# Joined score stacks, other store and load routes, and rings by lifetime in a gated attention and channel-mixing kernel

## The chip, the cores and the metric

The kernel runs on one core of a Trainium2 chip. The core has a matrix engine (PE, with its weight loads shown as PEld), three engines for elementwise work (DVE, ACT, POOL), a queue engine (SP) that here only issues transfers, and 16 DMA engines between the chip's memory and the core's buffer. Each engine works through its own instructions in order and waits on semaphores for the others.

The metric is the device time of one execution in microseconds (us), from the runs listed below; lower is better.

## The reference, cut to what matters

One sequence of 2048 rows of 512 goes through two branches, and a gate from the row itself mixes them:

```python
g = sigmoid((x * gate_w).sum(-1, keepdims=True))
# a: attention, 32 heads of 16, each row sees itself and the 255 rows before it
qkv = x @ wqkv                     # 512 -> 3 * 512
scores = q @ k.T * 16 ** -0.5      # masked to 0 <= i - j < 256
a = softmax(scores) @ v @ wo
# b: layernorm, 512 -> 1792, gelu, 1792 -> 512
b = gelu(layernorm(x) @ w1 + b1) @ w2 + b2
out = g * a + (1 - g) * b
```

All inputs are float32. The kernel multiplies in a reduced float32 form and makes up for it by splitting each operand into a high and a low part: a product is high x high + high x low + low x high, three matmuls instead of one.

## The kernel before

The kernel has three stages, and the order of every engine's instructions is the order in which the Python text emits them. A step counter drives it: `after(k, fn)` puts `fn` off by k steps, `tick()` advances by one and runs what is due. Every transfer but a few goes through SP's queue, in the order of emission.

**First stage (to about 146 us).** q, k and v are computed from x. q and k go to memory as *stacks* (`qk_out`): per head 50 rows of 2048 columns, 16 rows each of high, high and low parts for q and of high, low and high parts for k, so that one matmul over 48 rows gives the three-part product; two more rows (`gaps`) hold ones for k and later the negative row maximum, in two parts, for q. For three of the four head groups one of the two high copies is made later by a transfer from memory to memory (`double`, line 318). Row statistics, the gate and the normalized input of the second branch (`load_y`) are made here too.

**Second stage (to about 488 us).** The string `ORDER` fixes how four kinds of work alternate on PE: `S` (`s_pair`, line 353: scores, whose maximum DVE takes on line 367), `T` (`st_pair`, line 393: scores again, transposed, with the maximum subtracted inside the matmul; ACT takes exp on line 408, POOL masks on line 410), `P` (`pv`, line 417: the product with v, stored to `osc`), and `f` (`fill`: one pair of matmuls of `mlp1_unit`, line 611, the second branch's first product, stored to `hp`). Eight passes p take four heads each, as two couples `pr` of two heads. A pass has 16 blocks of 128 columns; `block(p, kb)` starts each with a tick. The stacks of a pass lie in four tiles, `qs[0]`, `qs[1]`, `ks[0]`, `ks[1]`, and are overwritten in place: every second block `load_stacks` (line 342) loads 256 columns for the next pass, one transfer for each of the four. `put_max` (line 372) sends four blocks' maxima through memory into the q tiles, in four transfers. The weights of `mlp1_unit` come with `load_w1`; `turn_w1` (line 542) makes a copy with the halves of the partitions exchanged. When no `T` is left, the late stores of `pv` and `mlp1_unit` (lines 440 and 641) go through ACT's queue instead of SP's.

Near the end of this stage `early_w2` loads the first four of 14 tiles of w2 and splits them, and two tiles of `hp` are loaded.

**Output stage (from about 488 us).** 56 items, four chunks of 512 rows by 14 tiles of the hidden layer: `mlp2` (line 840) does 12 matmuls for each (line 847). Ahead of them `load_h`, gelu on ACT and the split on DVE (line 686), and in the first chunk `load_w2`. Once in a chunk `attn_out` (line 797) loads the attention rows and the broadcast reciprocal sums (`rd`) for each of four groups (line 803), scales on POOL (line 806), splits, and multiplies with wo in four groups of 12 matmuls (line 824); ACT and DVE add the gate and the bias (826, 827). `mlp2` adds the second branch and stores (854, 856). Buffers come from two rings of tiles of 2 KB a partition: `e` (6) for the first loads, then one ring `t` (37) for everything, in order of request. The buffers of this stage lie over those of the second: a new tile waits for the last user of what lay there.

Of the kernel before, what the change touches and what calls it, by code (L numbers as in the profile page):

```python
# [49 lines left out]
LAG = 6  # L50
WARM = 10
# [13 lines left out]
def gated_mix_kernel(ctx, tc: tile.TileContext, xt, x2, wqk, wv, wo, xa, gw, w1, w2, b1, b2, out):  # L65
# [25 lines left out]
    def t2(dt=F32, shape=(128, 512)):  # L91
        return get("work", "t" if nt[0] > 0 else "e", abs(nt[0]), shape, dt)
# [59 lines left out]
    qkd = {(g, t): dram.tile([HG, 50, S], F32R, name=f"qk{g}_{t}") for g in range(NG) for t in range(2)}  # L152
# [4 lines left out]
    qs = [get("ring", f"q{j}", 1, (128, S), F32R) for j in range(2)]  # L157
    ks = [get("ring", f"k{j}", 1, (128, S), F32R) for j in range(2)]
# [42 lines left out]
    def gaps(g):  # L201
        for t in range(2):
            sp.dma_start(f32(view(qkd[g, t], [50 * S, HG], [S, 2], [1, S], off=48 * S)), f32(ks[0][112:128]))
# [100 lines left out]
    def qk_out(g, t, c, o):  # L304
        d = qkd[g, t]
# [4 lines left out]
        def send():  # L310
            for k, src in ((0, h), (1 + t, h), (2 - t, l)):
                if src is l or k == 0 or g == 0:
                    sp.dma_start(f32(view(d, [S, DH], [50 * S, HG], [1, C], off=k * DH * S + c * C)), f32(src))
            done.add(("qk", g, t, c))
# [3 lines left out]
    def double(g, c):  # L318
        for t in range(2):
            fr, to = (f32(view(qkd[g, t], [S, DH], [50 * S, HG], [1, C], off=k * DH * S + c * C)) for k in (0, 1 + t))  # L320
            sp.dma_start(to, fr)
# [20 lines left out]
    def load_stacks(p, a, n):  # L342
# [3 lines left out]
        for pr in range(2):  # L346
            for t, dst in ((1, ks[pr]), (0, qs[pr])):
                src = view(qkd[g, t], [S, 98], [1, n], off=(4 * j + 2 * pr) * 50 * S + a)
                sp.dma_start(f32(dst[14:112, a:a + n]), f32(src))
# [22 lines left out]
    def put_max(p, a):  # L372
# [8 lines left out]
        def rest():  # L381
            done.add(("m", p, a // 4))
            for pr in range(2):
                for e in range(2):
                    src = view(md, [2048, 2], [1, 512], off=(2 * pr + e) * 512)
                    sp.dma_start(f32(qs[pr][62 + 50 * e:64 + 50 * e, a * 128:a * 128 + 512]), f32(src))
# [30 lines left out]
    def pv(p, j, last):  # L417
# [17 lines left out]
        if j % 2:  # L435
# [3 lines left out]
            else:  # L439
                act.dma_start(to, s)  # L440
# [101 lines left out]
    def turn_w1(i):  # L542
        w1t[i, 1] = [wt(), wt()]
        for k in range(2):
            for e in range(2):
                sp.dma_start(f32(w1t[i, 1][k][64 * e:64 * e + 64]), f32(w1t[i, 0][k][64 - 64 * e:128 - 64 * e]))
        after(2, lambda: done.add(("w", i, 1)))
# [382 lines left out]
```

## Time and profile before

| what | value |
|---|---|
| median of 3 runs | 699.79 us (696.93 to 700.55) |
| the profiled execution | 699.06 us, span 697.3 us |
| granted PE clock, mean | 0.994 |
| PE busy | 682.1 us, 98% of the span |
| DVE, ACT, POOL busy | 466.0, 367.0, 273.6 us |
| moved by DMA | 137.95 MB, 198 GB/s |

Below, PE is the matmuls and PEld the weight loads; `out<-in` names the tiles; `[0.46 <-ACT t L131]` at a row's end is the idle time before it and what ended it; SPq and ACTq are issues of transfers by those queues. In the list of waits the three numbers are the total, how many, and the longest. In the chain of waits a row is a start, a duration and what ran or was in flight. The profile draws a matmul until its last result is out, so consecutive ones overlap; their pace is seen in their starts.

### The profile page before, as it was taken

How to read it: one execution, taken by the hardware profiler on the slowest of the kernel's cores; microseconds unless marked ns; L12 is line 12 of the kernel's file. 1: busy time of each engine (PE TensorE's matmuls, PEld its weight loads, DVE VectorE, ACT ScalarE, POOL GpSimd, SP SyncE). 2: the span in 40 equal slices, each digit the busy share in tenths (PEclk: the TensorE clock that was granted, in tenths of full speed). 3: DMA queues.
4: the chain of work that ended last, by engine and by line, in shares of the span. 5: the costliest groups of instructions: out<-in, count | busy, mean ns of one | idle time of the engine just before them, and what ended most of it. 6: DMA issues, size and time to landing. Idle time of an engine off the chain costs nothing.

```text
span 697.3 us, 16311 instructions
## 1 busy us (share of the span) xinstructions
PE 682.1 (98%) x5738; PEld 544.2 (78%) x5738; DVE 466.0 (67%) x1489; ACT 367.0 (53%) x586; POOL 273.6 (39%) x549
## 2 busy tenths in 40 slices
PE   9999999999999999999999999999988999999997
PEld 7877777877787778787887777787766888888885
DVE  5378865897887767767878778774574742824632
ACT  6332223367677576677767678778543322323221
POOL 7210029736465545566546457567020020020110
PEclk9999999999999999999999999999999999999999
DMA  8899876975776775568764655716883561641711
GB/s 271 265 310 303 287 247 227 302 219 169 246 220 199 239 218 163 171 216 265 197 197 148 207 171 162 216 64 220 295 246 102 161 190 50 210 141 50 244 45 60
DMA packets 91446, 137.95 MB, mean 198 GB/s; under 512 B 14852, under 2 KB 38596, under 8 KB 91236
## 3 DMA queue, kind: packets, MB, share of 16 engines
q1 hardware_dynamic: 90068, 135.20, 61.4%
q10 hardware_dynamic: 1296, 1.70, 0.7%
q8 instruction: 45, 0.74, 0.4%
q14 instruction: 37, 0.30, 0.1%
HBM read 81.53 MB, written 54.28 MB: 195 GB/s over the span
## 4 chain that ended last, share of the span: by engine, by line
PE 84%; DMA 9%; DVE 3%; ACT 2%; issue 1%; SPq 0%; POOL 0%; ACTq 0%; DVEq 0%; POOLq 0%
PE ps_b L623 21%; PE ps_a L847 17%; PE ps_b L425 12%; PE ps_d L300 9%; PE ps_b L406 7%; PE ps_o L824 6%; PE ps_b L362 6%; PE ps_d L336 4%; DMA t<-rd 3%; DMA t<-in_wo 2%; DMA t<-in_xa 1%; DMA q<-qk 1%; DMA t<-in_wqk 1%; PE ps_d L285 1%; DMA qk<-t 1%
## 5 line engine op out<-in xcount | busy, mean ns | idle before, releaser
L367 DVE CUSTOM_DVE_ANT_0 scr<-ps_b,wide 128x384 bf16<-128x384 f32 (+1 forms) x472 | 227.7, 530 | 67.8 <-PE ps_b L362 65.5
L623 PE MATMUL ps_b<-x,w 64*128 64x512 f32 x1344 | 209.8, 394 | 0.7 <-DVE t L128 0.7
L410 POOL TENSOR_SCALAR_AFFINE_SELECT p<-p 128x256 f32<-128x256 f32 x368 | 139.9, 411 | 130.1 <-ACT p L408 128.3
L408 ACT ACTIVATE p<-ps_b 128x768 f32<-128x768 f32 x192 | 146.6, 795 | 32.3 <-PE ps_b L406 25.3
L847 PE MATMUL ps_a<-x,t 128*128 128x512 f32 x648 | 150.0, 390 | 0.7 <-DVE t L686 0.5
L847 PEld LDWEIGHTS ps_a<-x,t 128*128 128x128 f32 x648 | 121.4, 188 | 27.4 <-ACT t L682 0.9
L623 PEld LDWEIGHTS ps_b<-x,w 64*128 64x128 f32 x1344 | 129.1, 187 | 10.2 <-DVE t L128 1.1
L406 PE MATMUL ps_b<-q,k 64*128 64x384 f32 (+5 forms) x512 | 90.1, 345 | 0.2 <-DVE mx L367 0.2
L806 POOL TENSOR_TENSOR t<-t,t 128x512 f32<-128x512 f32 x16 | 22.4, 1402 | 159.2 <-DMA t<-rd 121.7
L362 PE MATMUL ps_b<-k,q 62*128 62x384 f32 (+3 forms) x472 | 82.5, 338 | 2.3 <-DMA q<-qk 2.3
L131 ACT ACTIVATE t<-ps_b 128x256 f32<-128x256 f32 (+1 forms) x116 | 53.1, 487 | 46.6 <-PE ps_b L425 35.0
L425 PE MATMUL ps_b<-p,v 128*32 128x256 f32 (+1 forms) x1472 | 71.8, 330 | 0.0
L128 DVE TENSOR_TENSOR t<-t,t 128x512 fp32r<-128x512 f32 x66 | 49.6, 757 | 27.3 <-ACT t L131 24.1
L406 PEld LDWEIGHTS ps_b<-q,k 50*128 50x128 f32 (+1 forms) x512 | 49.4, 184 | 16.7 <-DVE mx L367 3.8
L425 PEld LDWEIGHTS ps_b<-p,v 128*32 128x32 f32 x1472 | 42.4, 110 | 23.3 <-issue 3.3
L362 PEld LDWEIGHTS ps_b<-k,q 62*128 62x128 f32 (+1 forms) x472 | 47.0, 186 | 13.3 <-issue 2.9
L410 POOL TENSOR_SCALAR_AFFINE_SELECT xq<-xq 128x256 f32<-128x256 f32 x112 | 43.2, 410 | 23.2 <-ACT xq L408 22.3
L408 ACT ACTIVATE xq<-ps_b 128x768 f32<-128x768 f32 (+1 forms) x64 | 44.3, 706 | 14.9 <-PE ps_b L406 13.0
L824 PE MATMUL ps_o<-wo,t 128*128 128x512 f32 x192 | 47.3, 399 | 4.1 <-ACT t L131 4.1
L827 DVE SCALAR_TENSOR_TENSOR us<-b2s,g,us 128x512 f32<-128x512 f32 x16 | 12.0, 752 | 58.5 <-ACT us L826 58.5
L682 ACT ACTIVATE t<-t,b1s 128x512 f32<-128x512 f32 x52 | 35.7, 714 | 22.4 <-DMA t<-hp 22.4
L131 ACT ACTIVATE t<-ps_d 128x512 fp32r<-128x512 f32 x32 | 18.9, 595 | 53.4 <-PE ps_d L300 44.5
(91 smaller groups left out, 734.0 us busy)
## 6 DMA issues: line engine op xcount, KB each, us to landing
qk<-t SPq DMA_DIRECT2D x72, 256.0 KB
hp<-t SPq DMA_DIRECT2D x54, 256.0 KB
t<-hp SPq DMA_DIRECT2D x52, 256.0 KB
k<-qk SPq DMA_DIRECT2D x112, 98.0 KB
q<-qk SPq DMA_DIRECT2D x112, 98.0 KB
osc<-t SPq DMA_DIRECT2D x30, 256.0 KB
w<-w SPq DMA_DIRECT2D x28, 256.0 KB
t<-in_w SPq DMA_DIRECT2D x26, 256.0 KB
```

Of the source, the lines that this page charges most:

```text
L128: eng.tensor_tensor(out=lo, in0=src, in1=f32(hi), op=ALU.subtract)
L131: act.activation(dst, src, AF.Copy)
L300: pe.matmul(o, a[:, dt * 128:(dt + 1) * 128], b[:, dt * C:(dt + 1) * C], start=n == 0, stop=n == 11)
L362: pe.matmul(o[:, e, :n], qs[pr][r:k, qb * 128:qb * 128 + 128], ks[pr][r:k, t0:t0 + n], start=True, stop=True)
L367: dve.tensor_tensor_reduce(out=sc[:, :n], in0=o[:, e, :n], in1=wide[:, 384 - n:], scale=1.0, scalar=NEG, op0=ALU.add, op1=ALU.max, accum_o ...
L406: pe.matmul(o[:, e, :w], ks[pr][r:k, kb * 128:kb * 128 + 128], qs[pr][r:k, kb * 128:kb * 128 + w], start=True, stop=True)
L408: act.activation(pt[:, :, :w], o[:, :, :w], AF.Exp, scale=0.25)
L410: pool.affine_select(out=pt[:, :, a:a + 128], in_=pt[:, :, a:a + 128], pattern=[[0, 2], [sgn, 128]], base=b, channel_multiplier=-sgn, comp ...
L425: pe.matmul(a[32 * h:32 * h + 32, at:at + w], vs[:, kb, v:v + 32], pts[p, kb][:, h, fr:fr + w], start=n == 0, stop=n == len(parts) - 1, sk ...
L623: pe.matmul(o[:, e], w[kt // 4][r:r + 64, k, m:m + 128], y[r:r + 64, a:a + C], start=n == 0, stop=n == 23)
L824: pe.matmul(a, hl[g][x][:, b * 128:b * 128 + 128], wos[g][:, k], start=n == 0, stop=n == 11)
L847: pe.matmul(accs[c][b], x[:, b * 128:(b + 1) * 128], w, start=f == 0 and n == 0, stop=f == FT - 1 and n == 2)
```

## The change

- q and k of both couples become one tile `qk` of 128 x 2 x 2 x 2048, and q and k of a group one tensor in memory. The columns of `wqk` are put into another order, so that the couples of a pass lie at a fixed step. `load_stacks` is one transfer of four slabs; `put_max` sends two transfers instead of four.
- `double` takes one of q and k at a time, at every second block of passes 0, 2 and 4 (before: both at once, at four blocks of passes 0, 1 and 3). `turn_w1` makes one of its four transfers a block (two for the last tile) instead of four at once.
- The late stores of `pv` and `mlp1_unit` go through POOL's queue.
- `attn_out` reads its rows with the 16 rows of a head outside and the 8 heads inside (before the other way round); the rows of wo are put into the same order. From the second chunk on it begins at item 0 instead of 2. The second pair of wo tiles is loaded one step earlier.
- `early_w2` takes six tiles and begins one block earlier.
- The output stage has rings by use, 8 tiles each: `e` for loads of `hp`, `r` for raw w2, `h` for split `hp`, `or` for attention rows and sums, `a` for raw wo and split attention rows. Loads in the item loop stand behind the splits and gelus, w2 two items further ahead.

```diff
+EW = 6
+EH = 7
+EB = 5
+AO = (2, 0)
+WO = (1, 2)
+GL = (1, 2, 3, 4)
+BUFS = {"e": 8, "r": 8, "h": 8, "or": 8, "a": 8}
...
-    def t2(dt=F32, shape=(128, 512)):
-        return get("work", "t" if nt[0] > 0 else "e", abs(nt[0]), shape, dt)
+    def t2(dt=F32, shape=(128, 512), tag="t"):
+        return get("work", tag, BUFS.get(tag) or nt[0], shape, dt)
...
-    qs = [get("ring", f"q{j}", 1, (128, S), F32R) for j in range(2)]
-    ks = [get("ring", f"k{j}", 1, (128, S), F32R) for j in range(2)]
+    qk = get("ring", "q", 1, (128, 2, 2, S), F32R)
+    qs, ks = ([qk[:, t, j] for j in range(2)] for t in range(2))
...
-    def double(g, c):
-        for t in range(2):
-            fr, to = (f32(view(qkd[g, t], [S, DH], [50 * S, HG], [1, C], off=k * DH * S + c * C)) for k in (0, 1 + t))
-            sp.dma_start(to, fr)
+    def double(g, c, t):
+        fr, to = (f32(view(qkd[g], [S, DH], [50 * S, HG], [1, C], off=t * QT + k * DH * S + c * C)) for k in (0, 1 + t))
+        sp.dma_start(to, fr)
...
-        for pr in range(2):
-            for t, dst in ((1, ks[pr]), (0, qs[pr])):
-                src = view(qkd[g, t], [S, 98], [1, n], off=(4 * j + 2 * pr) * 50 * S + a)
-                sp.dma_start(f32(dst[14:112, a:a + n]), f32(src))
+        src = view(qkd[g], [S, 98], [200 * S, 4], [1, n], off=j * 100 * S + a)
+        sp.dma_start(f32(qk[14:112].rearrange("p t j s -> p (t j) s")[:, :, a:a + n]), f32(src))
...
-            for pr in range(2):
-                for e in range(2):
-                    src = view(md, [2048, 2], [1, 512], off=(2 * pr + e) * 512)
-                    sp.dma_start(f32(qs[pr][62 + 50 * e:64 + 50 * e, a * 128:a * 128 + 512]), f32(src))
+            for e in range(2):
+                src = view(md, [2048, 2], [1024, 2], [1, 512], off=e * 512)
+                sp.dma_start(f32(qk[62 + 50 * e:64 + 50 * e, 0, :, a * 128:a * 128 + 512]), f32(src))
...
-                act.dma_start(to, s)
+                pool.dma_start(to, s)
...
+        for n in range(4):
+            if n < per:
+                turn(n // 2, n % 2)
+            else:
+                after(n // per, lambda n=n: turn(n // 2, n % 2))
+        after(2 + 3 // per, lambda: done.add(("w", i, 1)))
...
-                after(1, lambda: turn_w1(i + 1))
+                after(1, lambda: turn_w1(i + 1, 2 if 2 * i + 4 == FT else 1))
...
-                act.dma_start(hp[2 * cp + e, 2 * i + (e ^ v)], s)
+                pool.dma_start(hp[2 * cp + e, 2 * i + (e ^ v)], s)
...
-        if p in (0, 1, 3) and kb >= NB // 2 and kb % 2:
-            double((p + 3) // 2, kb // 2 - 4)
-        if p == 7 and kb == LAG:
+        if p in (0, 2, 4) and kb % 2:
+            double(p // 2 + 1, kb // 4, kb // 2 % 2)
+        if p == 7 and kb == EB:
             early_w2()
...
-    nt[0] = -6
+    nt[0] = 0
     waiting = {}
-    for f in range(2, 4):
+    for f in range(2, EH):
+        if f == 4:
+            for k in range(EW, EW + 2):
+                waiting["w", k] = load_w2(k)
         waiting[0, f] = load_h(0, f)
-    for f in range(4, 6):
-        waiting["w", f] = load_w2(f)
-    for f in range(4, 6):
-        waiting[0, f] = load_h(0, f)
-    nt[0] = 37
     flush()
...
-                ts.append(t2())
-                sp.dma_start(ts[g], view(d, [32 * S if step else C, HG], [step, DH], [1, C], off=off))
+                ts.append(t2(tag="or"))
+                sp.dma_start(ts[g], view(d, [step, DH], [32 * S if step else C, HG], [1, C], off=off))
...
-            after(1 + g, lambda g=g: loads(g))
-            after(4 + g, lambda g=g: scale(g))
-            after(5 + g, lambda g=g: parts(g))
-            after(6 + g, lambda g=g: low(g))
+            t = g + 1 if c else GL[g]
+            after(t, lambda g=g: loads(g))
+            after(t + 3, lambda g=g: scale(g))
+            after(t + 4, lambda g=g: parts(g))
+            after(t + 5, lambda g=g: low(g))
...
-        if n + 6 < FT:
-            waiting["w", n + 6] = load_w2(n + 6)
-        for k in (6, 7) if n == 0 else (n + 7,):
-            c, f = item(k)
-            if f >= 0:
-                waiting[c, f] = load_h(c, f)
...
+        if n + EW + 2 < FT:
+            waiting["w", n + EW + 2] = load_w2(n + EW + 2)
+        k = n + EH if n < 8 else n + 8
+        for k in (k,) if n != 8 else range(n + EH - 1, n + 9):
+            c, f = item(k)
+            if f >= 0:
+                waiting[c, f] = load_h(c, f)
         c, f = seq[n]
-        if f == 2:
+        if f == AO[c > 0]:
             attn_out(c)
```

More of the change, by code (lines that the diff above doesn't have):

```diff
@@ L151, in gated_mix_kernel @@
     hp = dram.tile([NCH, FT, 128, C], F32, name="hp")
-    qkd = {(g, t): dram.tile([HG, 50, S], F32R, name=f"qk{g}_{t}") for g in range(NG) for t in range(2)}
+    qkd = [dram.tile([2, HG, 50, S], F32R, name=f"qk{g}") for g in range(NG)]
+    QT = HG * 50 * S
     consts.tile([128, 112], F32, name="edge0")
@@ L202, in gaps @@
         for t in range(2):
-            sp.dma_start(f32(view(qkd[g, t], [50 * S, HG], [S, 2], [1, S], off=48 * S)), f32(ks[0][112:128]))
+            sp.dma_start(f32(view(qkd[g], [50 * S, HG], [S, 2], [1, S], off=t * QT + 48 * S)), f32(ks[0][112:128]))
     wq, wvs, xh, xl = {}, [], [], []
@@ L540, in load_w1, with turn_w1, turn @@
             after(3 + (eng is pool) + k, lambda k=k: part(k))
-    def turn_w1(i):
+    def turn_w1(i, per=4):
         w1t[i, 1] = [wt(), wt()]
[L544 to L547, printed above, removed]
+        def turn(k, e):
+            sp.dma_start(f32(w1t[i, 1][k][64 * e:64 * e + 64]), f32(w1t[i, 0][k][64 - 64 * e:128 - 64 * e]))
+        for n in range(4):
[4 more added lines that the diff above has]
+        after(2 + 3 // per, lambda: done.add(("w", i, 1)))
     open_psum({"x": 2}, {"d": 4})
@@ L646, in gated_mix_kernel, with late_tag @@
     w2s, wos, w2t, spare = {}, {}, [], []
+    def late_tag(tag):
+        return tag if nt[0] == 0 else "t"
     def load_w2(f):
@@ L653, in load_w2 @@
         w = w2s[f] = w2t[-1][:, f % 2 * 2 * C:f % 2 * 2 * C + 2 * C].rearrange("p (k n) -> p k n", k=2)
-        raw = t2()
+        raw = t2(tag=late_tag("r"))
         sp.dma_start(raw, w2[f])
@@ L658, in load_wo @@
     def load_wo(dt):
-        w, raw = get("work", "wo", DT, (128, 2, 512), F32R), t2()
+        w, raw = get("work", "wo", DT, (128, 2, 512), F32R), t2(tag="a")
         wos[dt] = w
@@ L664, in early_w2 @@
     def early_w2():
-        for n in range(4):
+        for n in range(EW):
             def go(n=n):
@@ L782, in gated_mix_kernel @@
         waiting[0, f] = (lambda: None), waiting[0, f][1]
-    for f in range(4, 6):
-        waiting.pop(("w", f))()
     pairs = dict(zip(ring, (("a0", "a1"), ("a2", "a3"), ("a4", "a5"), ("o0", "o1"))))
@@ L793, in gated_mix_kernel @@
     for n in range(2):
-        after(1 + 2 * n, lambda n=n: early_wo(2 * n))
+        after(WO[n], lambda n=n: early_wo(2 * n))
     us = {}
```

15 lines of the change are left out of this document (7 added, 8 removed).

## The prediction

> **What bounds the kernel now.** I read the page first, then the busy time by stretches, the chain of waits, and the timelines of PE and of SP's queue where PE loses time.
>
> ```profile
> span 697.3 us, 16311 instructions
> PE 682.1 (98%) x5738; PEld 544.2 (78%) x5738; DVE 466.0 (67%) x1489; ACT 367.0 (53%) x586; POOL 273.6 (39%) x549
> ...
> L847 PE MATMUL ps_a<-x,t 128*128 128x512 f32 x648 | 150.0, 390 | 0.7 <-DVE t L686 0.5
> ...
> L824 PE MATMUL ps_o<-wo,t 128*128 128x512 f32 x192 | 47.3, 399 | 4.1 <-ACT t L131 4.1
> ```
>
> PE is the bound, and the change takes no matmul away and leaves the order string alone. It can only win back time in which PE stands still or runs at half clock. The stretches (columns: PE, PEld, DVE, ACT, POOL busy, granted clock, DMA share, GB/s) show where that is:
>
> ```profile
> 225.00:240.00 15.00, 13.40 (x130) 10.67 (x128) 9.95 (x42) 8.90 (x16) 8.34 (x18) 0.89 0.75 239
> 250.00:255.00 5.00, 4.29 (x44) 3.50 (x42) 2.29 (x15) 3.65 (x5) 3.71 (x10) 1.00 0.95 297
> 488.00:495.00 7.00, 6.39 (x37) 4.82 (x30) 2.78 (x6) 4.52 (x9) 0.00 (x0) 1.00 0.77 241
> 515.00:530.00 15.00, 10.35 (x37) 7.49 (x36) 8.83 (x13) 5.90 (x10) 2.82 (x3) 0.89 0.64 199
> 529.00:690.00 161.00, 161.00 (x711) 133.32 (x711) 76.99 (x129) 45.02 (x70) 16.58 (x12) 1.00 0.39 123
> ```
>
> From 529 to 690 PE never stops: nothing to win there. Two places lose: the passage into the output stage (488 to 530), and two spots in the attention stage (225 to 240 and 250 to 255).
>
> **The passage.** PE's own rows, then the chain of waits:
>
> ```profile
> 487.99 0.40 PE L425 MATMUL ps_b<-xq,v 128*32 128x128 f32 x8
> ...
> 488.86 5.73 PE L847 MATMUL ps_a<-x,x 128*128 128x512 f32 x24 [0.46 <-ACT t L131]
> ```
> ```profile
> 689.90 2.88 PE L847 MATMUL ps_a<-x,t 128*128 128x512 f32 x12
> ```
> ```profile
> 490.73 2.99 DMA osc<-t
> 493.74 5.27 DMA t<-in_wo
> ...
> 504.24 9.24 DMA t<-rd
> 513.50 10.05 DMA t<-rd
> 523.68 1.27 POOL t L806
> 525.66 3.92 PE ps_o L824 x9
> 529.58 2.72 PE ps_a L847 x12
> ```
>
> At full speed 12 matmuls take 2.72 us, 0.227 each. The stage has 648 + 24 + 192 = 864 of them: 195.8 us, or 196.0 with the 0.16 by which the last one's end is drawn longer. It took from 488.86 to 692.78 (689.90 + 2.88), 203.9. So 7.9 us are lost inside it and 0.46 ahead of it: 8.4. Nine L824 matmuls at 525.66 take 3.92 instead of 2.04: the clock is half for a while after the long stop.
>
> What PE waits for at 521 to 525.66 is the fourth of the attention rows, scaled by the last `rd` broadcast, which landed at 523.55. Why so late? SP's queue:
>
> ```profile
> 484.61 0.90 SPq L655 DMA_DIRECT2D e<-in_w  x2
> 491.24 1.06 SPq L679 DMA_DIRECT2D e<-hp  x2
> 493.07 0.33 SPq L791 DMA_DIRECT2D b2s<-in_b  x1
> ```
> ```profile
> SPq L679 <- DMA hp<-t: 6.1, 2, 5.7
> ...
> SPq L791 <- DMA osc<-t: 0.8, 1, 0.8
> ```
>
> SP stands from 485.5 to 491.24 because a load waits for the landing of ACT's late store of `hp`; the bias row waits for the first late `osc` store, the `wo` load for the second (490.73 + 2.99 is within 0.02 of 493.74). In issue order each waits for the transfer eight places before it, although it shares no data with it. I read that as eight completion counters used in turn by SP's and ACT's transfers.
>
> **The change, part by part: the passage.**
>
> Late stores by POOL. ACT no longer issues four stores, and if POOL's do not share the counters, SP does not stop at 485.5. No row shows a POOL store. Bounds: from no wait at all to the same 5.7 us wait as for ACT's; I take none, as the stores leave the order of SP's and ACT's transfers. What then holds SP is memory: `b2s`, `wo` and its raw tiles now lie over `v`, free when the last L425 ends at 488.39. So `b2s` goes at about 488.4, not 493.07: 4.7 us earlier. Without ACT's issue between its two `hp` copies the first bank is free sooner: of the 0.46 some 0.4 go. Nothing waits for the stores: their rows are read tens of us later.
>
> The transfers from `b2s` to the last `rd` are 26 before and 25 after. Before they took 493.07 to 523.55, 1.17 us each. At that pace the last `rd` lands at 517.7. PE, unhindered, wants that row after eleven items of 12 matmuls and three of the attention product, at 488.45 + 135 x 0.227 = 519.1; POOL's 1.27 and a copy of some 0.6 (1.14 / 2 in a row below) bring it to 519.6. The stop shrinks from 4.5 to under 1, too short, I judge, for the half clock: the stop in 250 to 255 left it at 1.00.
>
> Output rows outside heads. Partitions are walked 16 x 8 instead of 8 x 16. Each `rd` took 9.24 and 10.05 from issue to landing, a `wo` load of the same 256 KB 5.27. If `rd` falls to that, the last one lands another 4.8 earlier, before 513, and the stop is gone. Bounds: 0 to 4.8 us earlier; both ends nearly remove the stop. The Trainium skill ("DMA: Bandwidth & Descriptors", "Why a DMA increments its semaphore by 16 and not by 1") says that a transfer is spread over the largest number of engines up to 16 that divides the slowest dimension of both patterns: 8 before, 16 after. By that rule the whole stop goes; by the rows alone up to 1 us stays. The 9 to 10 us against 5 agree with it.
>
> Two more early `w2` tiles, begun one block earlier (EW, EB). Two splits leave the passage:
>
> ```profile
> 492.40 1.14 ACT L131 ACTIVATE x<-e 128x512 fp32r<-128x512 f32 x2
> ...
> 493.05 1.29 DVE L128 TENSOR_TENSOR x<-e,x 128x512 fp32r<-128x512 f32 x2 [4.15 <-ACT x L131]
> ...
> 494.26 0.42 DVE L686 CAST t<-e 128x512 fp32r<-128x512 f32 x1
> ...
> 494.74 22.33 PE L847 MATMUL ps_a<-x,t 128*128 128x512 f32 x96
> ```
>
> The third `h` tile's cast (494.26) stood behind them and PE waited for it until 494.74; that loss, with the slow restart about 0.7, is inside the 8.4. The splits move into the last attention blocks, onto DVE (2 x 1.1 us by these rows). Cover gone, they cost 2.2.
>
> Rings by lifetime. `e` and `r` (16 tiles) fill the place of the merged q/k tile, free after the last score matmul, as before. The `h` ring of four pairs makes DVE wait for PE's item four back; behind it on DVE stand the next pairs, and SP's `h` loads wait for those. DVE still leads PE by three items, 8.2 us, for 1.1 us of work: cost 0, bounds 0 to 1.
>
> Output part two items earlier in later chunks (AO): the same matmuls. At the end it takes the last `us` update from in front of the final sums:
>
> ```profile
> 690.83 0.75 DVE L827 SCALAR_TENSOR_TENSOR us<-b2s,g,us 128x512 f32<-128x512 f32 x1 [4.69 <-ACT us L826]
> 691.50 2.85 DVE L854 SCALAR_TENSOR_TENSOR us<-ps_a,g,us 128x512 f32<-128x512 f32 x5
> ```
>
> The five end at 694.35, three whole ones (0.75 each) and two halves, 0.3 each by what is left. PE's end at 692.78 plus the halves would be 693.4. Gain 0 to 0.9; I take 0.4.
>
> **The change: the attention stage.**
>
> ```profile
> 228.62 0.23 PE L406 MATMUL ps_b<-q,k 64*128 64x128 f32 x2
> 230.44 0.44 PE L362 MATMUL ps_b<-k,q 62*128 62x384 f32 x2 [1.59 <-DMA q<-qk]
> ...
> 254.47 0.44 PE L362 MATMUL ps_b<-k,q 62*128 62x384 f32 x2 [0.71 <-DMA q<-qk]
> ```
> ```profile
> 216.01 1.24 SPq L321 DMA_DIRECT2D qk<-qk  x2
> ...
> 219.25 2.40 SPq L386 DMA_DIRECT2D q<-md  x4
> ...
> 244.52 2.76 SPq L546 DMA_DIRECT2D w<-w  x4
> ```
> ```profile
> 225.52 4.78 DMA q<-qk
> ...
> 250.66 3.67 DMA q<-qk
> ```
> ```profile
> L349 SPq DMA_DIRECT2D k<-qk x120: 307/342/1472, 26.2 to 451.6; - x120
> ```
>
> A score matmul waited 1.59 us for its stack, another 0.71. After the first the clock averaged 0.89 over 15 us: 1.65 us more. Sum 4.0. In both spots SP had been issuing without a pause: doublings, four `md` rows, weight copies, stores, then the stack in four pieces.
>
> The change turns 240 stack issues into 60 and 128 `md` issues into 64. At 0.34 each (the median above) and 0.6 (2.40 / 4) that is 100 us less of SP; were a joined issue as long as its four pieces, still 38. Doublings leave pass p = 1 (the spot at 216 to 230), and `w<-w` goes one a block: ahead of the stack piece issued at 250.66, three of four copies (2.07 us) and half an `md` set (1.2 of 2.40) leave SP's queue. The joined stack carries four pieces; the trace shows none. Bounds for its landing: 3.67 (one piece) to 6.4 (four issues, 1.6, and 4.78). Issued 3.3 us sooner, at 247.4, the stack that was wanted at 253.76 (254.47 - 0.71) has 6.4 us: enough up to the upper end, with nothing over. I take the whole 4.0; the other end is 0.
>
> Sum: 8.4 + 4.0 + 0.4 = 12.8, less 0.8 for waits that come up behind these (0.4 at the bank's release or a residue of the stop, 0.4 at the tightest stack): 12.0. The profiled execution took 699.06 (span 697.3 and 1.8 around it), which gives 687.1. It lay 0.7 under the median of the runs; I put the forecast at 687.5.
>
> A second rule, on the clock: the Trainium skill ("TensorE: Matmul & The Clock Gate", "HAM oscillation — how this bites in real kernels") wants no idle gap over about 3.4 us; here 1.59 us sufficed, and the measurement decides. By the rule the stack stalls would be worth 2.3, not 4.0, and the time 689.2.
>
> **Rivals.**
>
> Joined stacks are no earlier. One wait now covers four pieces, so the first pair of matmuls waits for the last byte. Were landing near 6.4, the stalls at 228 and 254 would stay: only 8.4 + 0.4 - 0.4 are won, 691.4. For it: the lead of 6.4 us at the tightest place. Against: SP's shorter queue.
>
> The passage is only half mended: POOL's stores do block the counters, or the engines were no limit. Then a stop of about 2 us and its 1.7 of half clock stay: 8.3 won, 691.5.
>
> The other side: coarse waits. q and k of both couples are one tile; if overlap is judged by the span between first and last address, every matmul after a stack load waits for its landing. From 56 loads in the attention stage at 3.67 that is 205 us: about 900 in all. It decides from the first L406 matmul behind a load. Against it:
>
> ```profile
> 27.88 1.83 SPq L313 DMA_DIRECT2D qk<-t  x3
> ```
>
> These three stores of one `qk` tile interleave their rows and are issued in 1.83 us, without waiting for each other's landing; patterns seem to be compared exactly.
>
> No change: a new queue takes the old one's place (SP behind DVE's ring, the joined stack behind `w2`), and what is won in one place is lost in another: 696 to 700.
>
> **How the numbers follow.** Forecast 0.64, late stacks 0.13, half-mended passage 0.08, no change 0.09, coarse waits 0.06. Under 0.5% (3.5 us, about what runs of this kernel can tell) is the no-change case with a little of the others. Faster 0.85, same 0.09, slower 0.06. The range: down to 684.5 (all 12.8, and runs that were 2 us under the profiled one), up to 694, which takes in either half case (691.4, 691.5) with 2.5 us of spread above it.
>
> **What would show it.** Right: no gap of PE over 1 us between 225 and 255 and none between 488 and 530; the clock 1.00 in both; SP's row of the bias load near 488; `rd` landing in about 5 us; the output stage near 197 us. Wrong: any L362 that waits for `q<-qk`, an L824 that waits for a copy behind POOL, or SP's queue waiting for a store of POOL.

## The result, and the profile after

The changed kernel takes 689.66 us (median of 4 runs, 689.20 to 689.74), the kernel before 700.17 us on the same chip (4 runs, 696.93 to 703.09): ratio 0.985, 95% interval 0.9806 to 0.9894. The forecast was 687.5, so the sign and the range held, and the kernel takes 2.2 us longer than forecast. The profiled execution of after took 689.74 us.

The page of after, first its span and engines, then the two groups of the output stage (busy time, mean ns of one, idle time ahead of them and what ended most of it):

```profile
span 687.8 us, 15950 instructions
PE 677.9 (99%) x5738; PEld 542.8 (79%) x5738; DVE 477.7 (69%) x1491; ACT 365.9 (53%) x584; POOL 279.9 (41%) x553
...
L857 PE MATMUL ps_a<-x,h 128*128 128x512 f32 x648 | 149.6, 389 | 0.5 <-DVE h L699 0.5
...
L833 PE MATMUL ps_o<-wo,a 128*128 128x512 f32 x192 | 47.3, 399 | 2.0 <-ACT a L138 2.0
```

The idle time ahead of the attention product fell from 4.1 to 2.0 us. It did not go. The stretches of after (columns as before: busy PE, PEld, DVE, ACT, POOL, granted clock, DMA share, GB/s) say where:

```profile
225.00:255.00 30.00, 30.00 (x370) 25.55 (x368) 23.81 (x101) 22.45 (x37) 18.23 (x45) 1.00 0.68 200
508.00:523.00 15.00, 12.46 (x46) 9.24 (x45) 11.57 (x16) 7.12 (x12) 3.40 (x3) 0.89 0.63 186
523.00:683.00 160.00, 160.00 (x708) 132.53 (x707) 83.91 (x130) 43.55 (x68) 18.25 (x12) 1.00 0.40 122
```

The attention stage is mended: PE is busy for the whole of 225 to 255 at full clock. The passage into the output stage is mended only at its start. From 508 to 523 PE still stands for 2.5 us and its clock averages 0.89, the same figure as in the worst stretch of before. PE's own rows there, then the chain of waits that leads to them:

```profile
482.33 0.40 PE L428 MATMUL ps_b<-xq,v 128*32 128x128 f32 x8
482.66 5.74 PE L857 MATMUL ps_a<-x,x 128*128 128x512 f32 x24
488.24 21.92 PE L857 MATMUL ps_a<-x,h 128*128 128x512 f32 x96
510.69 3.27 PE L857 MATMUL ps_a<-x,h 128*128 128x512 f32 x12 [0.53 <-DVE h L699]
513.80 0.84 PE L833 MATMUL ps_o<-wo,a 128*128 128x512 f32 x3
516.65 3.88 PE L833 MATMUL ps_o<-wo,a 128*128 128x512 f32 x9 [2.01 <-ACT a L138]
...
677.72 6.05 PE L857 MATMUL ps_a<-x,h 128*128 128x512 f32 x26
```
```profile
482.79 9.30 DMA b2s<-in_b
...
498.68 7.88 DMA or<-rd
...
506.57 7.96 DMA or<-rd
...
514.67 1.27 POOL or L815
```

The bank's release and the third cast are gone from the list of gaps: 24 matmuls follow the last `P` at once, and the next 96 follow those. What remains is the old stop, in the old place: three attention matmuls, then 2.01 us for the fourth row, then nine matmuls in 3.88 us at half clock. The cause has the old form too. The last `rd` broadcast lands at 506.57 + 7.96 = 514.53, and POOL's scaling and ACT's copy follow it. Counted from the end of the last `P` (482.33 + 0.40), that is 31.8 us; in before it was 523.55 - 488.39 = 35.2. So the passage moved the last `rd` by 3.4 us, where 5.9 (by the pace of before) to 10.6 (with faster `rd`) had been worked out. The output stage takes 201.1 us (482.66 to 677.72 + 6.05), against 203.9 before and 196.0 without a loss.

What SP did meanwhile, and the busy share of the 16 DMA engines:

```profile
482.79 0.36 SPq L800 DMA_DIRECT2D b2s<-in_b  x1
...
488.21 0.33 SPq L668 DMA_DIRECT2D r<-in_w  x1
492.11 0.33 SPq L692 DMA_DIRECT2D e<-hp  x1
```
```profile
486.00:488.00 2.00, 2.00 (x10) 1.66 (x9) 0.64 (x2) 1.04 (x2) 0.00 (x0) 1.00 1.00 333
489.00:490.00 1.00, 1.00 (x6) 0.84 (x5) 0.91 (x2) 0.00 (x0) 0.00 (x0) 1.00 1.04 406
...
505.00:510.00 5.00, 5.00 (x23) 3.94 (x21) 3.91 (x5) 2.57 (x5) 1.60 (x1) 1.00 1.06 266
```

SP no longer stands behind the late stores: the bias row goes out at 482.79, the moment its place is free. But it then lands only 9.30 us later, while from 486 to 510 the DMA engines are full (share 1.00 to 1.06 in these rows; in before SP's stop had left them at 0.77 from 488 to 495). SP stands again, later: from 488.5 to 492.1 a load of `hp` waits for the bias row, which went out eight places before it.

PE runs the same matmuls in all these kernels, up to the second chunk of the output stage in the same order, and those named here hold the same place in each; so the start of one and the same matmul can be compared between two traces. This is the lead of each kernel over the profiled execution of before, in us, at six such matmuls (named by their start in before); the runs below are explained in their sections:

```
                end of     ahead of    behind      last       behind the   last
                stage 1    the stacks  the stacks  passes     passage      matmuls
                146.15     228.15      260.15      480.17     540.08       690.13
after            1.21       0.87        5.42        5.66       9.01         9.01
after_again      1.30       1.30        5.86        6.04       9.24         9.24
walk_back        1.28       1.31        5.86        6.10       6.16         4.84
act_stores       1.02       0.05        4.59        4.89       6.82         6.82
stack_four       0.78       0.76        5.33        5.40       8.87         8.86
bunched          1.21       1.22        4.74        4.21       7.27         7.27
before_spread    1.16       0.78        5.32        4.69       3.33         3.33
bias_late        0.36       0.35        4.92        5.21       7.64         7.64
rows_early       0.64       0.59        5.17        5.33       8.66         8.66
bias_rows        1.27       1.25        5.83        6.05       9.52         9.52
deadline         0.81      -0.09        4.46        4.72       7.91         7.91
deadline2        0.23      -0.14        4.42        4.69      13.02        13.02
```

In after the stacks gave 4.55 us, the passage 3.35, the tail behind the last matmul another 0.53 (span 9.5 less, lead 9.0). The 0.9 that after leads by ahead of the stacks is no gain of the change: before_spread, which has no edit in the first stage, leads there by as much, and the kernels with all of it by anything from -0.14 to 1.31. No run takes the early w2 tiles, the rings or the earlier attention product of the later chunks alone; what is said of them below is read from the trace of after.

### The profile page after: what moved, and what is told of

Same layout as the page of the kernel before. It is cut to its first block, busy times and chain, and to the rows that moved or that the text cites. A ratio compares the mean times of both kernels' runs of the same rounds, so it can differ in the third digit from the quotient of the medians.

```text
span 687.8 us, 15950 instructions
## 1 busy us (share of the span) xinstructions
PE 677.9 (99%) x5738; PEld 542.8 (79%) x5738; DVE 477.7 (69%) x1491; ACT 365.9 (53%) x584; POOL 279.9 (41%) x553
## 4 chain that ended last, share of the span: by engine, by line
PE 86%; DMA 8%; DVE 3%; POOL 2%; issue 1%; ACT 0%; SPq 0%; DVEq 0%; POOLq 0%
PE ps_b L632 23%; PE ps_a L857 18%; PE ps_b L428 12%; PE ps_b L409 7%; PE ps_d L308 7%; PE ps_o L833 6%; PE ps_b L366 6%; PE ps_d L342 5%; DMA or<-rd 2%; DMA b2s<-in_b 1%; DMA t<-in_x 1%; DMA e<-hp 1%; DVE x L135 1%; PE ps_d L293 1%; POOL t L514 1%
## 5 line engine op out<-in xcount | busy, mean ns | idle before, releaser
L857 PE MATMUL ps_a<-x,h 128*128 128x512 f32 x648 | 149.6, 389 | 0.5 <-DVE h L699 0.5
L857 PEld LDWEIGHTS ps_a<-x,h 128*128 128x128 f32 x648 | 121.5, 188 | 26.5 <-ACT e L695 0.9
L632 PEld LDWEIGHTS ps_b<-x,w 64*128 64x128 f32 x1344 | 128.3, 186 | 10.3 <-DVE t L135 1.0
L409 PE MATMUL ps_b<-q 64*128 64x384 f32 (+5 forms) x512 | 90.0, 345 | 0.3 <-DVE mx L371 0.2
L815 POOL TENSOR_TENSOR or<-or,or 128x512 f32<-128x512 f32 x16 | 24.2, 1516 | 144.1 <-DMA or<-rd 140.9
L366 PE MATMUL ps_b<-q 62*128 62x384 f32 (+2 forms) x472 | 81.8, 336 | 0.0
L409 PEld LDWEIGHTS ps_b<-q 64*128 64x128 f32 (+1 forms) x512 | 49.3, 184 | 16.7 <-DVE mx L371 3.8
L366 PEld LDWEIGHTS ps_b<-q 62*128 62x128 f32 (+1 forms) x472 | 46.5, 185 | 10.0 <-issue 1.4
L833 PE MATMUL ps_o<-wo,a 128*128 128x512 f32 x192 | 47.3, 399 | 2.0 <-ACT a L138 2.0
L835 ACT ACTIVATE us<-ps_o,g 128x512 f32<-128x512 f32 x16 | 11.0, 690 | 66.6 <-PE ps_o L833 66.6
L833 PEld LDWEIGHTS ps_o<-wo,a 128*128 128x128 f32 x192 | 37.1, 194 | 10.2 <-ACT a L138 2.4
```

Source lines behind the costliest of these rows:

```text
L366: pe.matmul(o[:, e, :n], qs[pr][r:k, qb * 128:qb * 128 + 128], ks[pr][r:k, t0:t0 + n], start=True, stop=True)
L409: pe.matmul(o[:, e, :w], ks[pr][r:k, kb * 128:kb * 128 + 128], qs[pr][r:k, kb * 128:kb * 128 + w], start=True, stop=True)
L632: pe.matmul(o[:, e], w[kt // 4][r:r + 64, k, m:m + 128], y[r:r + 64, a:a + C], start=n == 0, stop=n == 23)
L833: pe.matmul(a, hl[g][x][:, b * 128:b * 128 + 128], wos[g][:, k], start=n == 0, stop=n == 11)
L857: pe.matmul(accs[c][b], x[:, b * 128:(b + 1) * 128], w, start=f == 0 and n == 0, stop=f == FT - 1 and n == 2)
```

## Experiments on the passage

Two explanations stood against each other. Mine: the eight counters and the engines that carry an `rd` hold the last row back, and both are mended. The rival: the bytes ahead of it hold it back, and then neither mends much.

**walk_back: heads outside again.** The rows of the attention output are walked 8 x 16 as before, with wo in the old order.

```diff
-                sp.dma_start(ts[g], view(d, [step, DH], [32 * S if step else C, HG], [1, C], off=off))
+                sp.dma_start(ts[g], view(d, [32 * S if step else C, HG], [step, DH], [1, C], off=off))
...
-        "in_wo": f(np.asarray(A_wo).reshape(NG, HG, DH, D).transpose(0, 2, 1, 3).reshape(DT, 128, D)),
+        "in_wo": f(np.asarray(A_wo).reshape(DT, 128, D)),
```

> The changed kernel, but the attention rows and the rd broadcasts are read with the heads outside again, and wo in its old order. Theory of the walk (the outer size of 8 keeps a transfer on part of the DMA engines): between the first osc load and the last rd landing 13.9 us become about 17.8, as before the change, so the last rd lands some 4 us later, PE's stop ahead of the attention product grows from 2.2 to about 6 us, and the time from 689.7 to about 693.5. Rival (the passage is bound by the bytes in flight, however they are walked): rd lands as in the changed kernel, stop 2.2, time 689.7 within 0.5.

Measured: 692.39 us (691.65 to 693.71), ratio 0.9897 (0.9856 to 0.9939). The rows of its chain of waits:

```profile
482.36 7.69 DMA b2s<-in_b
...
497.02 10.54 DMA or<-rd
507.58 9.51 DMA or<-rd
```
```profile
505.00:510.00 5.00, 4.73 (x21) 3.53 (x19) 2.32 (x4) 1.83 (x4) 1.29 (x1) 1.00 0.74 221
```

From the bias row's issue to the last `rd` it takes 34.7 us instead of 31.75, and the passage wins 0.06 us (6.10 to 6.16) where after wins 3.35; another 1.3 go in the later chunks. PE's stop does not become the 6 us that were expected: PE stands twice, 1.65 us for an `hp` pair and 2.57 us for the fourth row, with half clock behind each. The stretch from 505 to 510 bears the theory of the walk out in kind: with the heads outside the share of the engines is 0.74, in after it is 1.06. The walk is worth some 3 us in the passage. But its loads, 9.5 to 10.5 us with heads outside, come down to 7.9, not to 5.3.

**act_stores: the late stores by ACT again.**

```diff
-                pool.dma_start(to, s)
+                act.dma_start(to, s)
...
-                pool.dma_start(hp[2 * cp + e, 2 * i + (e ^ v)], s)
+                act.dma_start(hp[2 * cp + e, 2 * i + (e ^ v)], s)
```

> The changed kernel, but the four late stores go through ACT's queue again. Theory of the counters (a load on SP's queue waits for the transfer eight places before it, ACT's stores among them): SP stands for 3 to 5 us behind the landing of ACT's hp stores, the bias load goes 3 to 5 us later, the first PE stop (0.46 before the output stage) comes back, and the stop ahead of the attention product grows by 1 to 4 us: 691 to 694. Rival (the DMA engines are full anyway, and POOL's stores only add to what is ahead of rd): time 689.7 or up to 1 us less.

Measured: 690.14 us (688.29 to 691.42), ratio 0.9861 (0.9817 to 0.9906). Its SP rows, then its chain:

```profile
480.05 2.35 SPq L668 DMA_DIRECT2D r<-in_w  x2
485.88 1.96 SPq L692 DMA_DIRECT2D e<-hp  x3
488.83 0.33 SPq L800 DMA_DIRECT2D b2s<-in_b  x1
```
```profile
485.80 2.96 DMA osc<-t
...
507.81 8.16 DMA or<-rd
```

The reading of the queue was right: with ACT's stores SP stands from 482.4 to 485.88, and the bias row goes out when a late `osc` store has landed (485.80 + 2.96), 5.3 us behind the end of the last `P` (483.10 + 0.40) and not at once, as in after. Yet the last `rd` lands at 515.97, 32.5 us behind that end, where it is 31.8 in after and 31.2 in after_again, a second run of the changed kernel. So five us sooner at the head of the queue were worth 0.7 to 1.3 at its end. The passage wins 1.93 us here, and 3.35 and 3.20 in those two; 0.4 of the difference is the bank, where PE waits 0.40 for ACT's copy again. The time is not told apart from after's. The Trainium skill ("DMA: Bandwidth & Descriptors", "Issuing engines are not separate DMA queues") says that transfers run on the same 16 engines whichever engine starts them, so that starting them elsewhere saves the sequencer's time alone. The two traces agree with it as far as they go: of the five us that SP went sooner, most were gone at the last `rd`.

**bias_late, rows_early, bias_rows: two repairs, and both.** In bias_late the bias row, a broadcast of one row, goes out behind the `rd` loads; in rows_early the loads of the four attention rows, their scaling and their copies come up to two items sooner.

```diff
-    after(1, lambda: sp.dma_start(b2s, view(b2, [0, 128], [1, D])))
+    after(8, lambda: sp.dma_start(b2s, view(b2, [0, 128], [1, D])))
```
```diff
-GL = (1, 2, 3, 4)
+GL = (1, 1, 2, 2)
```

> The changed kernel, but the bias row b2s, one row of 2 KB read 128 times, is loaded seven items later, behind the rd broadcasts. Theory of broadcasts (reads of one row again and again hold the DMA engines longer than their bytes do; the bias load stood 9.3 us in flight, and for 3.9 us nothing else of SP's queue landed): the last rd lands 2 to 3.5 us earlier, PE's stop of 2.2 us and its half clock go, 3.9 us less: 685.8. Rival (bytes alone count): 0.65 us earlier, stop about 1.5, time 688.5 to 689.5.

> The changed kernel, but in the first chunk the four groups of attention rows are loaded at two items instead of four (GL 1, 1, 2, 2), so that four loads of w2 and hp stand behind the last rd, not ahead of it. Theory of full DMA engines (what is ahead in the queue sets when rd lands): the last rd lands 2.6 to 3.9 us earlier, the stop of 2.2 us and the half clock go: 684.8 to 686. Rival (the stop moves: the w2 and hp tiles that were put behind come late for items 11 to 13): the time within 0.7 of the changed kernel's.

> Both of these together. Full engines and broadcasts: no stop of PE between 482 and 688 but for restarts, 684 to 685.5. Rival: new stops at items 11 to 13, 686 or more.

The changed kernel ran beside them once more:

> The changed kernel itself, beside its variants on one chip. 689.7 within 1.5; in the profile the 2.2 us stop ahead of the attention product and 3.4 us of half clock after it.

Measured: after_again 689.58 us (688.47 to 691.53), ratio 0.9844 (0.9803 to 0.9885); bias_late 690.10, 0.9835 (0.9786 to 0.9885); rows_early 691.73, 0.9869 (0.9829 to 0.9910); bias_rows 690.05, 0.9846 (0.9803 to 0.9888). None is told apart from after. In bias_late's chain of waits the last `rd` lands no sooner, 515.71:

```profile
506.68 9.03 DMA or<-rd
```

One transfer of 25 out of the way moved nothing that can be seen; that this one row is read 128 times over was not the trouble. In rows_early the last `rd` landed at 509.15, 26.1 us behind the end of the last `P` instead of 31.8, and the stop moved. The chain's last `rd`, PE's rows, then ACT's:

```profile
501.56 7.59 DMA or<-rd
```
```profile
509.22 2.56 PE L857 MATMUL ps_a<-x,h 128*128 128x512 f32 x10 [0.96 <-DVE h L135]
513.30 4.45 PE L857 MATMUL ps_a<-x,h 128*128 128x512 f32 x12 [1.52 <-ACT x L138]
517.55 3.37 PE L833 MATMUL ps_o<-wo,a 128*128 128x512 f32 x12
```
```profile
510.94 0.63 ACT L138 ACTIVATE a<-or 128x512 fp32r<-128x512 f32 x1 [1.67 <-POOL or L815]
511.48 0.61 ACT L138 ACTIVATE x<-r 128x512 fp32r<-128x512 f32 x1
```

ACT takes its work in order. Its copies of the attention rows now wait for POOL in front of the split of a w2 tile (`x<-r`), and that tile is what PE waits for. The attention product itself (517.55) runs without a stop. In bias_rows, which has both edits, the last `rd` lands 26.7 us behind that end, and the same kind of stop is the only one of its passage:

```profile
512.97 4.35 PE L857 MATMUL ps_a<-x,h 128*128 128x512 f32 x12 [3.15 <-ACT x L138]
```

So there are two conditions: the rows must land early, and nothing urgent may stand behind their copies.

**sums_plain: is one row read many times over slow?** The `rd` loads read plain rows of `osc` in place of the sums.

```diff
-            for ts, d, step, off in ((os, osc, S, g * 256 * S + c * C), (rs, rds[c], 0, g * HG * C)):
+            for ts, d, step, off in ((os, osc, S, g * 256 * S + c * C), (rs, osc, S, max(g - 1, 0) * 256 * S + c * C)):
```

> The changed kernel, but the broadcast loads of the reciprocal sums read plain rows of osc in their place, as many bytes in as many pieces; so the division by the softmax sums is left out. Theory (reading one row many times over is what makes these loads slow): an rd-place load lands in about 5 us instead of 8, the last one by 511, the stop on the attention product falls from 2.0 us to under 0.5. Rival (full engines and 2 KB pieces of any row): landing within 0.7 us of the changed kernel's 514.5, stop 1.5 us or more.

It ran once, 692.18 us. The issue of the third load in `rd`'s place, and the scaling on POOL that waited for it:

```profile
503.34 0.52 SPq L812 DMA_DIRECT2D or<-osc  x1
```
```profile
511.96 1.79 POOL L815 TENSOR_TENSOR or<-or,or 128x512 f32<-128x512 f32 x1 [2.40 <-DMA or<-osc]
```

From issue to scaling it takes 8.6 us, in after with the sums 8.0 (502.65 to 510.64), and PE's stop on the attention product is 2.72 us. Repeated reading is not what makes these loads slow.

**deadline: the order by need.** Three things together: the bias row late, one w2 tile less of look-ahead here, rows loaded and scaled as in rows_early; but the copies of the first chunk's rows stand at the eighth and ninth item, behind the w2 splits that must not wait.

```diff
-GL = (1, 2, 3, 4)
+GL = (1, 1, 2, 2)
...
-    after(1, lambda: sp.dma_start(b2s, view(b2, [0, 128], [1, D])))
+    after(8, lambda: sp.dma_start(b2s, view(b2, [0, 128], [1, D])))
...
-            after(t + 4, lambda g=g: parts(g))
-            after(t + 5, lambda g=g: low(g))
+            after(t + 4 if c else 8, lambda g=g: parts(g))
+            after(t + 5 if c else 9, lambda g=g: low(g))
...
-        if n + EW + 2 < FT:
-            waiting["w", n + EW + 2] = load_w2(n + EW + 2)
+        if EW + 2 <= n + 7 < FT:
+            waiting["w", n + 7] = load_w2(n + 7)
```

> The changed kernel with the transfers of the passage put in the order in which they are needed: the bias row behind the loads of the attention rows, one w2 tile less of look-ahead there, and the four rescaled rows of the first chunk split one by one (loads in steps of 1, 1, 2, 2) from the eighth and ninth item on instead of in groups. Theory (the sixteen engines are full from 486 to 515, so only what stands ahead in bytes sets the last rd's landing): some 0.8 MB less ahead of it, at about 300 GB/s 2.5 us; the last rd lands at 510 to 512 instead of 514.5, no stop over 1 us, clock 1.00, 684.5 to 687. Rival (the copies of the rows on ACT and DVE stand ahead of the splits of w2, as in rows_early): the stop moves to PE's L857 and stays at 1.5 us or more, time 688.5 to 691.

Measured: 687.92 us (686.43 to 690.79), ratio 0.9793 (0.9739 to 0.9847). The last `rd` landed at 510.0, at the lower end of what the theory gave, and POOL scaled the last row at once. PE still stood, for neither theory's reason. The rows of POOL, of PE and of DVE:

```profile
510.14 1.29 POOL L815 TENSOR_TENSOR or<-or,or 128x512 f32<-128x512 f32 x1 [0.63 <-DMA or<-rd]
```
```profile
513.66 2.94 PE L833 MATMUL ps_o<-wo,a 128*128 128x512 f32 x8
518.15 2.60 PE L833 MATMUL ps_o<-wo,a 128*128 128x512 f32 x4 [1.55 <-DVE a L135]
```
```profile
515.67 0.69 DVE L135 TENSOR_TENSOR x<-r,x 128x512 fp32r<-128x512 f32 x1 [1.50 <-ACT x L138]
...
517.41 2.49 DVE L135 TENSOR_TENSOR a<-or,a 128x512 fp32r<-128x512 f32 x4
```

The low parts of rows that had been scaled by 511.43 began only at 517.41; they stood on DVE behind a w2 split and an `hp` pair of a later item: I had put them too far back.

**deadline2: the copies one item and two items sooner.** All parts of the first chunk's rows stand at the seventh item; the other edits of deadline stay. These lines are against deadline:

```diff
-            after(t + 4 if c else 8, lambda g=g: parts(g))
-            after(t + 5 if c else 9, lambda g=g: low(g))
+            after(t + 4 if c else 7, lambda g=g: parts(g))
+            after(t + 5 if c else 7, lambda g=g: low(g))
```

> The kernel of the run deadline, in which the four rows now land by 510 and are scaled by 511.4, but are copied to high and low parts 3 to 6 us later, because the copies stand two items further on; here both parts of all four rows stand at the seventh item, ahead of that item's w2 split. Theory (what is left of the stop, 1.55 us and the half clock after it, is only the place of the copies on ACT and DVE): no gap of PE over 0.6 us from 484 to 530, no half clock, output stage 197 us or less, 2.5 to 4 us less than deadline, ratio to the kernel before 0.974 to 0.978 (about 683.5 to 686). Rival (the copies now hold up the splits behind them, as in rows_early): a stop of 1 us or more on PE's L857, clock at half after it, ratio 0.979 or more.

Measured: 685.72 us (684.43 to 686.09), ratio 0.9774 (0.9749 to 0.9799): it beats both kernels (its slowest run, 686.09, is under the fastest of after and after_again, 688.47). Its stretch from before the passage to behind it, PE's rows, and SP's:

```profile
484.00:530.00 46.00, 46.00 (x204) 38.08 (x203) 30.03 (x47) 20.22 (x35) 7.38 (x8) 1.00 0.77 247
```
```profile
483.63 5.74 PE L857 MATMUL ps_a<-x,x 128*128 128x512 f32 x24
489.20 24.64 PE L857 MATMUL ps_a<-x,h 128*128 128x512 f32 x108
513.68 2.88 PE L833 MATMUL ps_o<-wo,a 128*128 128x512 f32 x12
...
675.75 4.01 PE L857 MATMUL ps_a<-x,h 128*128 128x512 f32 x17
```
```profile
501.60 0.51 SPq L812 DMA_DIRECT2D or<-rd  x1
...
508.71 0.33 SPq L800 DMA_DIRECT2D b2s<-in_b  x1
```

No gap and no half clock: the stage takes 483.63 to 675.75 + 4.01, 196.1 us, and the lead over before grows by 8.33 in the passage (4.69 to 13.02), of the 8.4 that the prediction found there. The last `rd` lands at 509.61, 25.9 us behind the end of the last `P`, against 31.8 in after. Six transfers of 256 KB that stood ahead of it in after now stand behind it: the bias row, three w2 tiles, two of `hp`. Rows that land early and copies in the right place together take the stop away, so these two were the cause of what was left of it.

How much each transfer weighs is less sure. rows_early, with four of the six behind (two w2 tiles, two of `hp`), had the last `rd` at 26.1 us, bias_rows, with the bias row as a fifth, at 26.7, deadline, with all six, at 26.3. So the four did nearly all of it, and the bias row and the last w2 tile brought nothing that stands out from the 0.6 us between after and after_again. Spread over six the 5.9 us are 0.98 each, over the four 1.4. What sets the pace is not separated either. SP lets a transfer go only when the one eight places before it has landed, and eight of 256 KB under way for 7.9 us each are 265 GB/s, the rate of after's stretch from 505 to 510 (266). The share of 1.06 there speaks for the engines as the limit, but no run changed the eight. By either reading the last row lands when what stands ahead of it is through.

## Experiments on the stacks

The prediction put the stalls down to SP's full queue in both spots, and gave the whole 4.0 to fewer issues and the spread together. The three runs here do each alone.

**stack_four: four transfers for a stack load, the spread kept.**

```diff
-        src = view(qkd[g], [S, 98], [200 * S, 4], [1, n], off=j * 100 * S + a)
-        sp.dma_start(f32(qk[14:112].rearrange("p t j s -> p (t j) s")[:, :, a:a + n]), f32(src))
+        for pr in range(2):
+            for t, dst in ((1, ks[pr]), (0, qs[pr])):
+                src = view(qkd[g], [S, 98], [1, n], off=t * QT + (2 * pr + j) * 100 * S + a)
+                sp.dma_start(f32(dst[14:112, a:a + n]), f32(src))
```

> The changed kernel, but each stack load is four transfers again, from the joined tensor into the joined tile; doublings and weight copies stay spread. Theory of traffic (the two stalls came from doublings and weight copies that stood ahead of the stack in the queue and in flight): PE waits for no stack, time 689.7 within 0.5, with some 1.2 us more of SP's time for each load. Rival (the number of issues on SP's queue made the stalls): the waits of L366 for q<-qk come back, 1 to 2.3 us and half clock after them, 691 to 694.

**bunched: the joined stacks, but doublings and w1 copies at their old places.**

```diff
-                after(1, lambda: turn_w1(i + 1, 2 if 2 * i + 4 == FT else 1))
+                after(1, lambda: turn_w1(i + 1))
...
-        if p in (0, 2, 4) and kb % 2:
-            double(p // 2 + 1, kb // 4, kb // 2 % 2)
+        if p in (0, 1, 3) and kb >= NB // 2 and kb % 2:
+            for t in range(2):
+                double((p + 3) // 2, kb // 2 - 4, t)
```

> The changed kernel, but the doublings stand at their old places (passes 0, 1 and 3, two at a time) and the weight copies go four at once. Theory of traffic: the stalls near 228 and 249 come back with the joined stack, at least that near 249, where the stack now lands 1 us ahead of its use and would be 2 us later: 1 to 4.5 us, 690.7 to 694. Rival (the number of stack issues made the stalls): no wait for a stack, 689.7 within 0.5.

**before_spread: the kernel before, with that spread alone.**

```diff
-        if p in (0, 1, 3) and kb >= NB // 2 and kb % 2:
-            double((p + 3) // 2, kb // 2 - 4)
+        if p in (0, 2, 4) and kb % 2:
+            double(p // 2 + 1, kb // 4, (kb // 2 % 2,))
...
-                after(1, lambda: turn_w1(i + 1))
+                after(1, lambda: turn_w1(i + 1, 2 if 2 * i + 4 == FT else 1))
```

> The kernel before with only the spread of the doublings of q and k and of the copies of w1; stacks still go in four transfers per couple and the passage is as it was. Theory (traffic ahead of the stacks made them late, their number did not): PE waits for no stack over 0.3 us, the clock is 1.00 from 225 to 255, some 4 us less than before, 695.5 to 696.5. Rival (spread and joined stacks are both needed): one of the two waits stays, at most 1.5 us less than before, 698.5 or more.

Measured: stack_four 687.39 us (686.74 to 689.42), ratio 0.9821 (0.9772 to 0.9869); bunched 690.76 (688.20 to 691.81), 0.9867 (0.9821 to 0.9912); before_spread 695.81 (694.00 to 697.20), 0.9911 (0.9877 to 0.9946). The stretch over both spots of stack_four, then of before_spread; the late score matmul of bunched among PE's rows, then one of before_spread behind the two spots:

```profile
225.00:255.00 30.00, 30.00 (x370) 25.37 (x369) 23.81 (x101) 22.44 (x36) 18.13 (x44) 1.00 0.65 201
```
```profile
225.00:260.00 35.00, 35.00 (x416) 29.96 (x416) 27.99 (x118) 25.71 (x40) 21.08 (x52) 1.00 0.66 205
```
```profile
249.72 0.45 PE L366 MATMUL ps_b<-q 62*128 62x384 f32 x2 [0.80 <-DMA q<-qk]
```
```profile
273.12 0.44 PE L362 MATMUL ps_b<-k,q 62*128 62x384 f32 x2 [0.36 <-DMA q<-qk]
```

At the two spots the spread alone does it all. With it PE waits there for no stack, whether a load is one transfer or four, and the kernel before wins 4.54 us between the two points (0.78 to 5.32), as after does (0.87 to 5.42). before_spread keeps all 240 stack issues and all 128 `md` issues, so fewer of them were not needed. The joined transfers without the spread mend the first spot alone: bunched wins 3.63 us there (its lead grows from 1.22 to 4.85, read at the matmul that starts at 236.07 in before), then waits 0.80 us at the second, where the four w1 copies stand in front, and 0.48 at another near 344. So at the first spot either remedy is enough; at the second the spread is needed. No run takes the doublings and the w1 copies apart. The joining buys nothing that shows in the time: stack_four's median is 2.2 us under after's, and the intervals of the two ratios overlap.

Behind the two spots before_spread loses again, which neither after nor stack_four does: 0.63 us up to the last passes (5.32 to 4.69), with one wait of 0.36 for a stack, and 1.36 in the passage (4.69 to 3.33), where PE stops for 1.10 and 3.91 us and the clock averages 0.77 from 515 to 530, against 0.89 in before. Why was not followed.

## Why the prediction was right or wrong

**Attention stage: right in size, the reason too wide.** 4.55 us won where 4.0 was taken, both waits gone, clock 1.00. But the step "The change turns 240 stack issues into 60 and 128 `md` issues into 64", with its 38 to 100 us less of SP, isn't what mended it: before_spread keeps all these issues and waits at neither spot. The part of that step which moved doublings and copies away was enough. The rival with late joined stacks fell: no score matmul of after waits for a stack.

**Late stores by POOL: the mechanism right, its worth wrong.** The counters were read rightly: the bias row went at 482.79, the moment the last `P` ended, and act_stores brings SP's stop back. The step that failed is the next one: the transfers from `b2s` to the last `rd` were given before's 1.17 us each from the earlier start. That pace had SP's stop in it, in which the engines ran at 0.77. Without the stop they fill, and the five us at the head of the queue became 0.7 to 1.3 at its end.

**The walk: right in kind, mis-sized.** "If `rd` falls to that", 5.27 us, was the term that failed: 7.88 and 7.96 were measured. The row of 5.27 came from a stretch where the engines were not full (share 0.81 from 493.74 to 499.01). Among the full engines of after a `wo` load too took 10.3 us: it was issued at 483.20, and the w2 load eight places behind it went at 493.49. Walk_back gives the walk about 3 us in the passage, not 4.8 on top of the 5.9. By the rule of the Trainium skill that the prediction cites, on how many engines carry a transfer, the whole stop was to go. The shares, 0.74 with the heads outside and 1.06 with the rows outside, are in the direction of that rule, but the stop stayed, and the measurement decides.

**The half-mended rival** named this end (a stop of about 2 us and its half clock) with a chance of 0.08 and 691.5 us. Its conditions were wrong: the stores did not block the counters, and the walk did help. A third way, full engines, led there. One of the signs that the prediction named for being wrong did come: the attention product waits for a copy behind POOL. The measured 689.66 lies nearer to the two half cases (691.4, 691.5) than to the forecast, and the range had been drawn to take both in; that the time fell inside it does not speak for the view of the passage. The profile of before had the hint: a DMA share of 0.77 from 488 to 495 while SP stood still for half of it leaves little to win by starting sooner.

**The other terms.** The bank's release gave 0.53 where 0.4 was taken, the third cast 0.72 for 0.7 (the lead grows by these from the matmul at 488.00 in before to the one at 488.86, and from 494.20 to 500.13), the tail 0.53 for 0.4. The stop ahead of the attention product (0.53 in the row at 510.69, counted with the 8.4) stayed: DVE's split of a w2 tile, in front of that `hp` pair, waited for ACT, and ACT for POOL's scaling of an attention row. No score matmul waited for a whole tile, so the coarse waits fell; nor did the time stay as it was. Of the 0.8 held back, the 0.4 for a residue of the stop was far too little, and no wait at the tightest stack used the other 0.4.

**The sum.** 12.0 net was forecast; 8.7 came from the change (4.55 + 0.24 between the stacks and the passage + 3.35 + 0.53), and 0.9 of first-stage scatter on top of it made the profiled 9.5. That 0.9 is luck. Nothing of the 8.4 in the passage was imaginary: deadline2 wins 8.33 of it. What failed was the view that two edits to who issues and how the rows are walked would free it, where the order of the transfers was the limit.

## What to carry to other kernels

Before a stall is put down to a late issue, read the DMA share of the stretch between issue and need: if the engines are near full, starting sooner buys little, and the question is which transfers ahead of the late one can wait. When the late data then comes early, look at each in-order engine on its way, because a copy that waits for it blocks what stands behind, and a copy put off too far is late itself. A remedy made of several edits wants each edit alone on the chip: here the spread of some copies did what the larger joining of transfers was thought to do.

## What the runs showed of the hardware

- A stop of PE of 1.5 to 2 us was enough, in these traces, for about 3.4 us at half clock. In after nine matmuls at 516.65 took 3.88 us behind a 2.01 us wait, and a mean clock of 0.89 over 15 us is 3.3 us at half; in deadline a wait of 1.55 did it, in rows_early one of 1.52. The waits of 0.40 to 0.80 shown above did not, nor one of 1.10 us in before_spread (ahead of 513.58). The Trainium skill ("TensorE: Matmul & The Clock Gate", "HAM oscillation — how this bites in real kernels") sets the bar at idle gaps of about 3.4 us; the rows here put it lower.
- At a DMA share of 1.04 to 1.06 the rate was 406 GB/s while weights, `hp` and plain stores went, and 266 while half the transfers were attention rows and sums of the same 256 KB. sums_plain rules out the repeated reading as its reason; what else it is, the distance in memory between the pieces of an attention row for one, stays open.
- A transfer from SP waited for the landing of the one eight places before it in two more places: behind the bias row in after (482.79 + 9.30 is 492.09, and the `hp` load goes at 492.11), and behind ACT's store in act_stores. POOL's four stores did not take a place, but took 8.1 and 9.4 us (medians) to land among the loads.
